# Attention block: the weighted values of every second unit in two halves, and another order of a pair's products

## The chip, the cores and the metric

The kernel runs on one core of one Trainium2 chip. The metric is the device time of one execution in microseconds (us); the time of a kernel is the median of several executions. A second source is one execution under the hardware profiler, which records every instruction with its start, its duration and what it waited for.

## The reference

The input `x` has 2048 rows of 512 values. The reference adds a full softmax attention with 32 heads of 16 channels, and after it a gated mixer:

```python
def _A_ref(x, wqkv, wo):
    H = 32; Dh = D // H
    qkv = (x @ wqkv).reshape(B, S, 3, H, Dh)...
    scores = jnp.einsum("bhqd,bhkd->bhqk", q, k) * Dh ** -0.5
    p = _softmax(scores, axis=-1)
    o = jnp.einsum("bhqk,bhkd->bhqd", p, v)
    return o... @ wo
...
h = x + _A_ref(_layernorm(x, axis=-1), A_wqkv, A_wo)
h2 = h + _B_ref(_layernorm(h, axis=-1), B_w_in, B_w_sp, B_b_sp, B_w_out)
```

Everything is float32. The change touches the attention alone: the scores, the row maxima that the softmax subtracts, and the product of the weights with the values.

## The kernel before

**Stages.** The first stage normalizes `x` and makes queries, keys and values; the second is the attention, which this text is about; then come the product with `wo`, the mixer's first product, its product over the sequence and its last product.

**Units of attention.** Four heads are handled together (a group `hg`, 8 in all), 512 queries at a time (a block `qb`, 4 in all), 128 keys at a time (`kb`, 16 in all). One such piece is a unit; there are 512 units, and the loop at L744 takes two per turn: `kb` even and `kb1`, the odd one behind it. Such a turn is called a pair here, and eight pairs make a block of queries.

**Scores and weights.** `score` (L665) makes the scores of two of the four heads: two TensorE products of 512 columns into one tile `s` of two PSUM banks (L673), and one ScalarE exponential over both banks, into `pt` (L676). The two products stand in different rows of the array: head `t=0` uses rows 0 to 49, `t=1` rows 64 to 113. Products in the upper and in the lower rows can run beside each other. The pool `ps_s` has two tiles, so the third `score` of a pair writes where the first one was, and waits for its exponential.

**Weighted values.** `weigh` (L679) multiplies the weights of the four heads with the values: four products, each with all 128 rows of the array but 32 of its columns, into the four quarters of one PSUM bank `pv`. The operands are plain float32, and the compiler makes two instructions of each, so one `weigh` is eight instructions (L684). The sum over the 16 units of a block stays in `pv`; `gather` (L687) then copies it out, half of it on VectorE (L690) and half on ScalarE (L694), and `weigh` of the next block's first unit has to wait for both copies.

**Maxima.** The softmax needs the maximum of each query's scores ahead of time. `max_pair` (L207) makes them for 128 queries and two heads per pair, eleven pairs (`LEAD`) ahead of their use. It returns eight steps. Each is one product of 512 columns in the upper (`t=0`) or lower (`t=1`) rows into one of three single banks (`ps_m`, numbers 0 to 2), and what reads that bank: six are read by a VectorE maximum (L230), `minus` by a ScalarE absolute value into `ab` (L235), and `plus` by a VectorE custom operation that takes `ab` too (L239). The first four keys' blocks of the upper head are taken through sum and difference, which is why that head has `plus`, `minus` and the blocks 2 and 3 only. Every eighth pair, `last` also reduces the maxima on VectorE (L245), and in the pair behind it `max_rows` (L255) transposes them (L259) and sends them into the query tile by DMA. `invert` (L644, a VectorE reciprocal at L648) runs once in a block.

**Order.** In this part the order of TensorE, ScalarE, VectorE and SyncE is the order of the program (`manual_schedule`, L743). A pair issues, on TensorE (upper, lower: the rows used; the bank of a maximum in brackets):

| place | before |
|---|---|
| 1 | `S0` upper, lower; `Sb` upper, lower (the scores of unit `kb`, both head pairs) |
| 2 | `four0` lower (2), `two` upper (0) |
| 3 | `weigh` of the pair before's second unit |
| 4 | `minus` upper (1), `four1` lower (2) |
| 5 | `Sc` upper, lower; `four2` lower (0); `Sd` upper, lower (the scores of unit `kb1`) |
| 6 | `four3` lower (1), `plus` upper (2) |
| 7 | `weigh` of this pair's first unit |
| 8 | `last` upper (1): block 3 of the upper head |

The names in this table are used from here on; `S0`, `Sb`, `Sc`, `Sd` stand for the four calls of `score`. In the first pair of a block, `gather` is called between 4's two products. From unit 490 on there are no maxima left, and the steps do nothing; products of the next stage (`more_h`) take their place.

Of the kernel before, what the change touches and what calls it, by code (L numbers as in the profile page):

```python
# [8 lines left out]
F32 = mybir.dt.float32  # L9
# [3 lines left out]
AF = mybir.ActivationFunctionType  # L13
# [5 lines left out]
P = 128  # L19
# [3 lines left out]
DH = 16  # L23
# [3 lines left out]
NB = S // P  # L27
HB = NB // 2
NQ = S // 512
DB = D // P  # L30
HG = H // 4
# [17 lines left out]
def block_kernel(ctx: ExitStack, tc: tile.TileContext, x, wqkv, wo, w_in, w_sp4, b_sp, w_out, out):  # L49
# [154 lines left out]
            return more[i]()  # L204
        return ps_m.tile([P, 512], F32, name=f"m{i}")

    def max_pair(m):  # L207

        g, i = divmod(m, 8)
        hg, qb = divmod(g, NQ)
        q, k, w = qst[g], kst[hg % 2], uvs[hg % 2]
        if i == 0:
            mx[g] = sm.tile([P, 16, 4], F32, name="mx")
            nc.gpsimd.memset(mx[g][:, :8, 3:], LOW)
        c, p = slice(i % 4 * P, i % 4 * P + P), i // 4
        at = lambda t, e: mx[g][:, t * 8 + i, e:e + 1]  # L220

        def scores(t, keys, b):
            r = slice(RG * t, RG * t + KS)
            acc = bank(b)
            nc.tensor.matmul(acc, q[r, p, c], keys[r, p], start=True, stop=True)  # L225
            return acc

        def one(t, e, b):
            acc = scores(t, k[:, :, 512 * e:512 * e + 512], b)
            nc.vector.reduce_max(at(t, e if t else e - 1), acc, axis=AX.X)  # L230

        def minus(b):
            acc = scores(0, w[:, :, 512:], b)
            ab[0] = sm.tile([P, 512], F32, name="ab")
            nc.scalar.activation(ab[0], acc, AF.Abs)  # L235

        def plus(b):
            acc = scores(0, w[:, :, :512], b)
            nc.vector.tensor_tensor_reduce(ab[0], acc, ab[0], 0.5, LOW, ALU.add, ALU.max, at(0, 0))  # L239

        def last(b):
            one(0, 3, b)
            if i == 7:
                nm = sm.tile([P, 2, 8], F32, name="nm")
                nc.vector.tensor_reduce(nm.rearrange("p t i -> p (t i)"), mx.pop(g), axis=AX.X,  # L245
                                        op=ALU.max, negate=True)
                parts = sm.tile([P, 2, 2, 8], F32R, name="mparts")
                split(parts[:, :, 0], parts[:, :, 1], nm, "pool", "pool")
                turned[0] = (g, parts)

        ab = {}
        four = [lambda b, e=e: one(1, e, b) for e in range(4)]
        return [four[0], lambda b: one(0, 2, b), minus, four[1], four[2], four[3], plus, last]

    def max_rows():  # L255

# [398 lines left out]
    with ExitStack() as at:  # L655
# [6 lines left out]
        ps_s = at.enter_context(tc.tile_pool(name="ps_s", bufs=2, space=PSUM))  # L662
        pv = {}

        def score(hg, qb, kb, p):  # L665

            q, k = qst[hg * NQ + qb], kst[hg % 2]
            turn[0] += len(later)
            pool = later[0] if later and turn[0] % 3 == 2 else ps_s
            s = pool.tile([P, 2, 512], F32, name="s")  # L670
            for t in range(2):
                r = slice(RG * t, RG * t + KM)
                nc.tensor.matmul(s[:, t, :], k[r, p, kb * P:(kb + 1) * P], q[r, p, :],  # L673
                                 start=True, stop=True)
            t = pp.tile([P, 2, 512], F32, name="pt")
            nc.scalar.activation(t, s, AF.Exp, scale=DH ** -0.5)  # L676
            return t

        def weigh(hg, qb, kb, pts):  # L679
            if kb == 0:  # L680
                pv[0] = ps_v.tile([P, 512], F32, name="pv")
            for j in range(4):
                c = (4 * kb + j) * VW
                nc.tensor.matmul(pv[0][32 * j:32 * j + 32, :], vst[hg % 2][:, c:c + 32],  # L684
                                 pts[j % 2][:, j // 2, :], start=kb == 0, stop=kb == NB - 1)

        def gather(hg, qb, pool=sm):  # L687

            o = pp.tile([P, 512], F32, name="o", bufs=1)
            nc.vector.tensor_copy(o[:, :256], pv[0][:, :256])  # L690
            if pool is sm and later:
                nc.vector.tensor_copy(o[:, 256:], pv[0][:, 256:])
            else:
                nc.scalar.activation(o[:, 256:], pv[0][:, 256:], AF.Copy)  # L694
            cols = slice(qb * 512, (qb + 1) * 512)
            sums = pool.tile([P, 16], F32, name="sums")
            for j in range(4):
                h = head(hg, j % 2, j // 2)
                nc.sync.dma_start(o_scr[h * DH:(h + 1) * DH, cols], o[32 * j:32 * j + DH, :])
                nc.sync.dma_start(sums[32 * j:32 * j + 32, :], o[32 * j + DH:32 * j + VW, :])  # L700
            sums_[0] = (hg, cols, sums, pool)
# [18 lines left out]
        def more_h(k):  # L720

            for _ in range(k):
                if not pieces:
                    sb = h_rows[len(hns)]
                    acc = later[0].tile([P, 512], F32, name="h")
                    pieces.extend([sb, acc, h_products(sb, acc)])
                sb, acc, products = pieces
                next(products)
                made[0] += 1
                if made[0] % (3 * DB):  # L730
                    continue
                pieces.clear()
                add_h(sb, acc)
                split_o(h_rows[len(hns) + 1], *("pool", "pool") if hns else [None])
                mv, rs = scale_h(sb)
                hns[sb] = e2.tile([P, D], F32, name="hn", bufs=3)
                nc.vector.tensor_scalar(hns[sb], xrs.pop(sb), mv[:, 0:1], rs,
                                        op0=ALU.subtract, op1=ALU.mult)
# [4 lines left out]
        with tc.manual_schedule(engines={E.PE, E.Activation, E.DVE, E.SP}):  # L743
            for n in range(0, len(units), 2):  # L744
                (hg, qb, kb), (_, _, kb1) = units[n:n + 2]
                if hg + 1 < HG and n % 64 < 24 and n % 4 == 0:
                    load_k(hg + 1, [n % 64 // 4])
                if hg + 1 < HG and n % 64 < 12 and n % 4 == 2:
                    load_uv(hg + 1, [n % 64 // 4])
                if hg + 1 < HG and n % 64 == 30:  # L750
                    load_v(hg + 1)
                if kb == 2 and n // NB + 3 < HG * NQ:
                    load_q(n // NB + 3)
                steps = max_pair(m) if m < 8 * HG * NQ else []
                m += 1
                if not steps and not later:
                    maxima.close()
                    later.append(attn.enter_context(
                        tc.tile_pool(name="ps_l", bufs=1, space=PSUM, side="right")))
                step = lambda b: steps and steps.pop(0)(b)  # L760
                pts = [score(hg, qb, kb, 0), score(hg, qb, kb, 1)]
                step(2)
                step(0)
                if prev is None:

                    pv[0] = ps_v.tile([P, 512], F32, name="pv")
                    for j in range(4):
                        nc.tensor.matmul(pv[0][32 * j:32 * j + 32, :], vst[0][:, :32],
                                         vst[0][:, :512], start=True, stop=True)
                else:  # L770
                    weigh(*prev)
                step(1)
                if kb == 0 and n:
                    gather(*units[n - 1][:2])
                step(2)
                pts1 = [score(hg, qb, kb1, 0)]
                step(0)
                pts1.append(score(hg, qb, kb1, 1))
                step(1)
                step(2)  # L780
                if n >= 490:
                    more_h(2 + (n < 494))
                weigh(hg, qb, kb, pts)
                if turned:
                    max_rows()
                step(1)
                prev = (hg, qb, kb1, pts1)
                if kb == 6 and n > NB:
                    invert()
                if n % 32 == 16 and n < 6 * 32:  # L790
                    load_weights(n // 32)
                if n in (476, 482, 492, 504):
                    load_o(h_rows[(476, 482, 492, 504).index(n)])
                if n == 482:
                    split_o(h_rows[0], "pool", "pool")
            weigh(*prev)
            gather(*prev[:2], e2)
# [186 lines left out]
    with ExitStack() as fin:  # L984
# [29 lines left out]
        def product(acc, a, b, blocks=range(HB)):  # L1014
            for k in blocks:
                mm3(acc, a[0][:, k, :], a[1][:, k, :], b[0][:, k, :], b[1][:, k, :],
                    k == 0, k == HB - 1)
# [299 lines left out]
```

## Time and profile before

| | us |
|---|---|
| median of 3 runs | 1863.78 (1863.67 to 1863.93) |
| the profiled execution's own time | 1863.55 |
| its span in the profile | 1861.7 |
| first and last absolute value `ab` of the attention loop's 245 pairs with maxima | 170.4 and 1360.2 |
| VectorE busy between 800 and 1000 us | 183.80 of 200 |
| ScalarE busy there | 176.64 of 200 |

The span reaches from the first to the last instruction that the profiler recorded. An engine's busy time counts the time in which at least one of its instructions runs. The TensorE row says little by itself: matmuls overlap, and the ends of those rows are modelled, so the engine seems to be busy all the time. Their starts are recorded, and differences between starts are what the reading goes by. In a timeline, several instructions of a kind that follow one another are one row, with the start of the first and a count; PEld is the loading of a product's weights into the array, ahead of the product.

### The profile page before, as it was taken

The numbers are of one execution on the slowest core, as the hardware profiler recorded it, in microseconds if no ns is written. First come the engines' busy times: TensorE is split into PE (matmuls) and PEld (weight loads), VectorE is DVE, ScalarE is ACT, GpSimd is POOL, SyncE is SP. The second block draws the span as 40 slices with busy tenths as digits, with TensorE's granted clock in tenths as the row PEclk, the third lists the DMA queues.
The fourth block names the chain that finished last, engine by engine and source line by source line (L and its number), as shares of the span: only waits on it lengthen the run. The fifth ranks groups of instructions, "written<-read, shape, count | busy, mean of one in ns | idle before, by whom it ended". The sixth has DMA issues, their size and how long they took to land.

```text
span 1861.7 us, 31964 instructions
## 1 busy us (share of the span) xinstructions
PE 1852.8 (100%) x11410; PEld 1047.3 (56%) x11410; DVE 1530.4 (82%) x3060; ACT 1317.8 (71%) x1696; POOL 225.7 (12%) x305
## 2 busy tenths in 40 slices
PE   9999999999999999999999999999999999999999
PEld 6775444444444444444444444444437889999998
DVE  6487999999999999999999999999935766877664
ACT  3224888888888888888888888888895444434221
POOL 2241000011010100000000000000001756001111
PEclk9999999999999999999999999999999999999999
DMA  6688111221120121022011112100123555768662
GB/s 192 193 191 197 41 24 30 48 53 28 39 57 15 49 44 25 13 51 40 13 39 32 23 29 50 25 14 13 30 56 108 175 160 166 226 186 264 212 191 94
DMA packets 148743, 159.90 MB, mean 86 GB/s; under 512 B 63096, under 2 KB 93320, under 8 KB 147240
## 3 DMA queue, kind: packets, MB, share of 16 engines
q1 hardware_dynamic: 143800, 146.44, 29.7%
q10 hardware_dynamic: 4752, 11.41, 1.6%
q8 instruction: 90, 1.47, 0.3%
q14 instruction: 69, 0.57, 0.1%
q0 software_dynamic: 32, 0.01, 0.0%
HBM read 101.26 MB, written 55.61 MB: 84 GB/s over the span
## 4 chain that ended last, share of the span: by engine, by line
PE 98%; DVE 1%; issue 0%; ACT 0%; DMA 0%; SPq 0%; POOL 0%; POOLq 0%; DVEq 0%; ACTq 0%
PE pv L684 27%; PE m L225 26%; PE s L673 13%; PE acc L96 5%; PE acc L98 5%; PE acc L97 5%; PE g L98 4%; PE g L97 4%; PE g L96 4%; PE acc L617 2%; PE tp L1189 1%; PE h L617 0%; PE tp L885 0%; PE acc L1210 0%; PE tp L369 0%
## 5 line engine op out<-in xcount | busy, mean ns | idle before, releaser
L676 ACT ACTIVATE pt<-s 128x1024 f32<-128x1024 f32 x1024 | 994.1, 1030 | 141.6 <-PE s L673 139.2
L230 DVE TENSOR_REDUCE mx<-m 128x1 f32<-128x512 f32 x1508 | 956.6, 684 | 99.7 <-PE m L225 56.6
L225 PE MATMUL m<-kst,qst 48*128 48x512 f32 x1508 | 605.1, 447 | 0.0
L684 PE MATMUL pv<-pt,vst 128*32 128x512 f32 x4096 | 545.8, 605 | 0.0
L673 PE MATMUL s<-qst,kst 50*128 50x512 f32 x2048 | 465.1, 428 | 0.0
L225 PEld LDWEIGHTS m<-kst,qst 48*128 48x128 f32 x1508 | 262.7, 184 | 316.2 <-DVE mx L230 221.4
L673 PEld LDWEIGHTS s<-qst,kst 50*128 50x128 f32 x2048 | 222.6, 185 | 53.9 <-ACT pt L676 29.8
L225 PE MATMUL m<-uvs,qst 48*128 48x512 f32 x497 | 246.5, 496 | 0.0
L225 PEld LDWEIGHTS m<-uvs,qst 48*128 48x128 f32 x497 | 90.8, 183 | 205.4 <-DVE mx L230 204.6
L684 PEld LDWEIGHTS pv<-pt,vst 128*32 128x32 f32 x4096 | 80.8, 108 | 158.2 <-issue 155.5
L239 DVE CUSTOM_DVE_ANT_0 ab<-m,ab 128x512 f32<-128x512 f32 x249 | 169.6, 681 | 0.0
L235 ACT ACTIVATE ab<-m 128x512 f32<-128x512 f32 x248 | 149.3, 602 | 4.1 <-PE m L225 4.0
L90 POOL CAST mparts<-nm 128x16 fp32r<-128x16 f32 x32 | 6.3, 197 | 880.2 <-DVE nm L245 880.2
L825 ACT ACTIVATE ws<-a 128x512 fp32r<-128x512 f32 x80 | 45.8, 621 | 50.0 <-PE g L98 23.6
L904 ACT ACTIVATE z<-acc 128x464 f32<-128x464 f32 (+2 forms) x64 | 27.6, 456 | 65.3 <-PE acc L98 63.3
L96 PE MATMUL acc<-wi,hT 128*128 128x464 f32 (+2 forms) x196 | 72.8, 371 | 0.0
L98 PE MATMUL acc<-wi,hT 128*128 128x464 f32 (+2 forms) x196 | 71.8, 366 | 0.0
L97 PE MATMUL acc<-wi,hT 128*128 128x464 f32 (+2 forms) x196 | 71.6, 365 | 0.0
L826 DVE TENSOR_TENSOR ws<-a,ws 128x512 fp32r<-128x512 f32 x80 | 56.1, 745 | 13.1 <-ACT ws L825 13.0
L96 PE MATMUL g<-b,ws 128*128 128x344 f32 x192 | 62.6, 326 | 0.0
L88 ACT ACTIVATE part<-acc 128x512 fp32r<-128x512 f32 x32 | 19.1, 598 | 60.8 <-PE acc L98 56.0
L98 PE MATMUL g<-t,ws 128*128 128x344 f32 x192 | 61.3, 319 | 0.0
(200 smaller groups left out, 2121.2 us busy)
## 6 DMA issues: line engine op xcount, KB each, us to landing
a<-in_w_sp SPq DMA_DIRECT2D x80, 256.0 KB
qst<-q_scr SPq DMA_DIRECT2D x192, 64.0 KB
z_scr<-z ACTq DMA_DIRECT2D x32, 344.0 KB
kst<-k_scr SPq DMA_DIRECT2D x42, 256.0 KB
k_scr<-part SPq DMA_DIRECT2D x16, 512.0 KB
q_scr<-part SPq DMA_DIRECT2D x16, 512.0 KB
z<-z_scr SPq DMA_DIRECT2D x14, 344.0 KB
b<-z_scr SPq DMA_DIRECT2D x24, 172.0 KB
```

The lines of the kernel that those rows point to most:

```text
L96: nc.tensor.matmul(ps, lh, rh, start=first, stop=False)
L97: nc.tensor.matmul(ps, lh, rl, start=False, stop=False)
L98: nc.tensor.matmul(ps, ll, rh, start=False, stop=last)
L225: nc.tensor.matmul(acc, q[r, p, c], keys[r, p], start=True, stop=True)
L230: nc.vector.reduce_max(at(t, e if t else e - 1), acc, axis=AX.X)
L235: nc.scalar.activation(ab[0], acc, AF.Abs)
L239: nc.vector.tensor_tensor_reduce(ab[0], acc, ab[0], 0.5, LOW, ALU.add, ALU.max, at(0, 0))
L673: nc.tensor.matmul(s[:, t, :], k[r, p, kb * P:(kb + 1) * P], q[r, p, :], start=True, stop=True)
L676: nc.scalar.activation(t, s, AF.Exp, scale=DH ** -0.5)
L684: nc.tensor.matmul(pv[0][32 * j:32 * j + 32, :], vst[hg % 2][:, c:c + 32], pts[j % 2][:, j // 2, :], start=kb == 0, stop=kb == NB - 1)
L825: nc.scalar.activation(hi, src, AF.Copy)
L826: (nc.gpsimd if el == "pool" else nc.vector).tensor_sub(lo, src, hi.bitcast(F32))
```

## The change

`max_pair` gets an argument `late`, with which it returns the same eight products in another order, with `four3` as the last one in place of the upper head's block 3 (here `last`). `score` is taken apart into `scores_of`, which returns two functions: the first makes the upper product, the second the lower product and the exponential. `weigh` takes a range of columns. The loop's body, for pairs that have maxima, is written anew; for the others it is as before, without the empty steps. What a pair issues on TensorE becomes:

| place | after |
|---|---|
| 1 | `minus` upper (2); `S0` upper, lower; `four0` lower (1); `Sb` upper |
| 2 | `weigh` of the pair before's second unit, columns 0 to 255 (all columns in the first pair of a block) |
| 3 | `two` upper (0); `Sb` lower; `last` upper (1); `four1` lower (2); `Sc` upper, lower |
| 4 | `weigh` of the same unit, columns 256 to 511 (nothing in the first pair of a block) |
| 5 | `Sd` upper; `four2` lower (0); `plus` upper (1); `Sd` lower |
| 6 | `weigh` of this pair's first unit, whole |
| 7 | `four3` lower (0) |

`gather` now stands between `last` and `four1`. VectorE's order in a pair becomes `four0`, `two`, `last`, `four1`, `four2`, `plus`, `four3` (before: `four0`, `two`, `four1`, `four2`, `four3`, `plus`, `last`), and ScalarE's becomes `minus`, `S0`, `Sb`, `Sc`, `Sd` (before: `S0`, `Sb`, `minus`, `Sc`, `Sd`).

```diff
-    def max_pair(m):
+    def max_pair(m, late=False):
...
-        return [four[0], lambda b: one(0, 2, b), minus, four[1], four[2], four[3], plus, last]
+        two = lambda b: one(0, 2, b)
+        if late:
+            return [minus, four[0], two, lambda b: one(0, 3, b), four[1], four[2], plus,
+                    lambda b: last(b, 1, 3)]
+        return [four[0], two, minus, four[1], four[2], four[3], plus, lambda b: last(b, 0, 3)]
...
-        def weigh(hg, qb, kb, pts):
+        def weigh(hg, qb, kb, pts, cols=slice(0, 512)):
...
-                nc.tensor.matmul(pv[0][32 * j:32 * j + 32, :], vst[hg % 2][:, c:c + 32],
-                                 pts[j % 2][:, j // 2, :], start=kb == 0, stop=kb == NB - 1)
+                nc.tensor.matmul(pv[0][32 * j:32 * j + 32, cols], vst[hg % 2][:, c:c + 32],
+                                 pts[j % 2][:, j // 2, cols], start=kb == 0,
+                                 stop=kb == NB - 1 and cols.stop == 512)
...
-                pts = [score(hg, qb, kb, 0), score(hg, qb, kb, 1)]
-                step(2)
-                step(0)
...
-                    weigh(*prev)
-                step(1)
-                if kb == 0 and n:
-                    gather(*units[n - 1][:2])
-                step(2)
-                pts1 = [score(hg, qb, kb1, 0)]
-                step(0)
-                pts1.append(score(hg, qb, kb1, 1))
-                step(1)
-                step(2)
...
-                weigh(hg, qb, kb, pts)
-                if turned:
-                    max_rows()
-                step(1)
+                if steps:
+                    step = lambda b: steps.pop(0)(b)
+                    step(2)
+                    pts = [score(hg, qb, kb, 0)]
+                    step(1)
+                    first, second = scores_of(hg, qb, kb, 1)
+                    first()
...
+                        weigh(*prev, *[slice(0, 256)] * (kb > 0))
+                    step(0)
+                    pts.append(second())
+                    step(1)
+                    if kb == 0 and n:
+                        gather(*units[n - 1][:2])
+                    step(2)
+                    pts1 = [score(hg, qb, kb1, 0)]
+                    if kb:
+                        weigh(*prev, slice(256, 512))
+                    first, second = scores_of(hg, qb, kb1, 1)
+                    first()
+                    step(0)
+                    step(1)
+                    pts1.append(second())
+                    weigh(hg, qb, kb, pts)
+                    if turned:
+                        max_rows()
+                    step(0)
```

More of the change, by code (lines that the diff above doesn't have):

```diff
@@ L239, in plus, with last @@
             nc.vector.tensor_tensor_reduce(ab[0], acc, ab[0], 0.5, LOW, ALU.add, ALU.max, at(0, 0))
-        def last(b):
-            one(0, 3, b)
+        def last(b, *which):
+            one(*which, b)
             if i == 7:
@@ L663, in block_kernel, with score, scores_of @@
         pv = {}
-        def score(hg, qb, kb, p):
+        def score(*unit):
+            first, second = scores_of(*unit)
+            first()
+            return second()
+        def scores_of(hg, qb, kb, p):
             q, k = qst[hg * NQ + qb], kst[hg % 2]
@@ L670, in score, with product @@
             s = pool.tile([P, 2, 512], F32, name="s")
-            for t in range(2):
+            def product(t):
                 r = slice(RG * t, RG * t + KM)
@@ L674, in score, with second @@
                                  start=True, stop=True)
-            t = pp.tile([P, 2, 512], F32, name="pt")
-            nc.scalar.activation(t, s, AF.Exp, scale=DH ** -0.5)
-            return t
-        def weigh(hg, qb, kb, pts):
+            def second():
+                product(1)
+                t = pp.tile([P, 2, 512], F32, name="pt")
+                nc.scalar.activation(t, s, AF.Exp, scale=DH ** -0.5)
+                return t
+            return lambda: product(0), second
+        def weigh(hg, qb, kb, pts, cols=slice(0, 512)):
             if kb == 0:
@@ L753, in block_kernel @@
                     load_q(n // NB + 3)
-                steps = max_pair(m) if m < 8 * HG * NQ else []
+                steps = max_pair(m, True) if m < 8 * HG * NQ else []
                 m += 1
@@ L759, in block_kernel @@
                         tc.tile_pool(name="ps_l", bufs=1, space=PSUM, side="right")))
-                step = lambda b: steps and steps.pop(0)(b)
-                pts = [score(hg, qb, kb, 0), score(hg, qb, kb, 1)]
-                step(2)
-                step(0)
[L764 to L769, printed above, removed]
+                if steps:
[5 more added lines that the diff above has]
+                    first()
+                    if prev is None:
+                        pv[0] = ps_v.tile([P, 512], F32, name="pv")
+                        for j in range(4):
+                            nc.tensor.matmul(pv[0][32 * j:32 * j + 32, :], vst[0][:, :32],
+                                             vst[0][:, :512], start=True, stop=True)
+                    else:
+                        weigh(*prev, *[slice(0, 256)] * (kb > 0))
[9 more added lines that the diff above has]
+                    first, second = scores_of(hg, qb, kb1, 1)
+                    first()
+                    step(0)
[5 more added lines that the diff above has]
+                    step(0)
@@ L770, in block_kernel @@
                 else:
+                    pts = [score(hg, qb, kb, 0), score(hg, qb, kb, 1)]
                     weigh(*prev)
-                step(1)
-                if kb == 0 and n:
-                    gather(*units[n - 1][:2])
-                step(2)
-                pts1 = [score(hg, qb, kb1, 0)]
-                step(0)
-                pts1.append(score(hg, qb, kb1, 1))
-                step(1)
-                step(2)
-                if n >= 490:
-                    more_h(2 + (n < 494))
@@ L783, in block_kernel @@
-                weigh(hg, qb, kb, pts)
-                if turned:
-                    max_rows()
-                step(1)
+                    if kb == 0:
+                        gather(*units[n - 1][:2])
+                    pts1 = [score(hg, qb, kb1, 0), score(hg, qb, kb1, 1)]
+                    if n >= 490:
+                        more_h(2 + (n < 494))
+                    weigh(hg, qb, kb, pts)
+                    if turned:
+                        max_rows()
                 prev = (hg, qb, kb1, pts1)
```

## The prediction

> **What bounds the kernel now.** I read the page first.
>
> ```profile
> PE 1852.8 (100%) x11410; PEld 1047.3 (56%) x11410; DVE 1530.4 (82%) x3060; ACT 1317.8 (71%) x1696; POOL 225.7 (12%) x305
> PE 98%; DVE 1%; issue 0%; ACT 0%; DMA 0%; SPq 0%; POOL 0%; POOLq 0%; DVEq 0%; ACTq 0%
> L676 ACT ACTIVATE pt<-s 128x1024 f32<-128x1024 f32 x1024 | 994.1, 1030 | 141.6 <-PE s L673 139.2
> L230 DVE TENSOR_REDUCE mx<-m 128x1 f32<-128x512 f32 x1508 | 956.6, 684 | 99.7 <-PE m L225 56.6
> L684 PE MATMUL pv<-pt,vst 128*32 128x512 f32 x4096 | 545.8, 605 | 0.0
> ```
>
> The chain of waits says 98% TensorE, which is no finding: the matmul rows overlap. So I took the stage between 800 and 1000 us, by stretches and then by the timeline of each engine. All three engines are nearly full, and none quite:
>
> ```profile
> 800.00:1000.00 200.00, 200.00 (x1314) 82.60 (x1312) 183.80 (x349) 176.64 (x211) 3.37 (x16) 1.00 0.17 36
> ```
>
> The columns are the stretch, its length, then busy us and instructions of PE, PEld, DVE, ACT, POOL, then the granted clock (full), the DMA share and GB/s. TensorE, in order of time:
>
> ```profile
> 800.72 1.06 PE L684 MATMUL pv<-pt,vst 128*32 128x512 f32 x8
> 801.72 0.50 PE L225 MATMUL m<-kst,qst 48*128 48x512 f32 x1
> 801.72 0.96 PE L673 MATMUL s<-qst,kst 50*128 50x512 f32 x4
> 802.34 0.58 PE L225 MATMUL m<-kst,qst 48*128 48x512 f32 x2
> 802.85 1.07 PE L684 MATMUL pv<-pt,vst 128*32 128x512 f32 x8
> 803.85 0.50 PE L225 MATMUL m<-uvs,qst 48*128 48x512 f32 x1
> 803.85 0.49 PE L225 MATMUL m<-kst,qst 48*128 48x512 f32 x1
> 804.19 0.40 PE L673 MATMUL s<-qst,kst 50*128 50x512 f32 x2
> 804.42 0.40 PE L225 MATMUL m<-kst,qst 48*128 48x512 f32 x1
> 804.55 0.51 PE L673 MATMUL s<-qst,kst 50*128 50x512 f32 x2
> 805.04 0.50 PE L225 MATMUL m<-kst,qst 48*128 48x512 f32 x1
> 805.17 0.49 PE L225 MATMUL m<-uvs,qst 48*128 48x512 f32 x1
> 805.59 1.06 PE L684 MATMUL pv<-pt,vst 128*32 128x512 f32 x8
> ```
>
> A pair takes 805.59 - 800.72 = 4.87 us: `weigh` 1.00, the row-half products `last` to `two` 1.13, `weigh` 1.00, the products `minus` to `plus` 1.74. Upper and lower products start side by side (803.85 twice). Behind a first product the next in the same rows comes after 0.34 us (803.85 to 804.19), each further one after 0.24 (804.19 to 804.42); `weigh` starts 0.42 behind a lone first product (805.17 to 805.59). A stage of k products in the busier rows so takes 0.10 + 0.24k + 0.08: 1.14 for the four upper ones of the first stage (measured 1.13), 1.38 for the five lower ones of the second, where 1.74 are seen. The 0.36 us between are waits, and the other engines' rows name them:
>
> ```profile
> 804.55 0.19 PEld L673 LDWEIGHTS s<-qst,kst 50*128 50x128 f32 x2 [0.17 <-ACT pt L676]
> 805.04 0.18 PEld L225 LDWEIGHTS m<-kst,qst 48*128 48x128 f32 x1 [0.30 <-ACT ab L235]
> 805.16 0.18 PEld L225 LDWEIGHTS m<-uvs,qst 48*128 48x128 f32 x1
> 802.56 1.94 ACT L676 ACTIVATE pt<-s 128x1024 f32<-128x1024 f32 x2 [0.61 <-PE s L673]
> 803.48 1.02 ACT L676 ACTIVATE pt<-s 128x1024 f32<-128x1024 f32 x1
> 804.38 0.60 ACT L235 ACTIVATE ab<-m 128x512 f32<-128x512 f32 x1
> 804.88 1.94 ACT L676 ACTIVATE pt<-s 128x1024 f32<-128x1024 f32 x2
> 802.25 1.89 DVE L230 TENSOR_REDUCE mx<-m 128x1 f32<-128x512 f32 x3 [0.20 <-PE s L673]
> 804.42 1.89 DVE L230 TENSOR_REDUCE mx<-m 128x1 f32<-128x512 f32 x3 [0.28 <-PE m L225]
> 806.22 0.68 DVE L239 CUSTOM_DVE_ANT_0 ab<-m,ab 128x512 f32<-128x512 f32 x1
> ```
>
> `four1` starts at 803.85, its maximum at 804.42 (0.57 later), which ends near 805.11, and `plus`, which wants the bank, loads at 805.16. So today's loop is: `weigh`, `four1`, its maximum, `plus`, `weigh`, the first stage; 1.00 + 0.57 + 0.69 + 0.05 + 0.42 + 1.00 + 1.13 = 4.86, against 4.87 seen. The same steps also give what I need below: a first product's reader starts 0.53 behind it (`minus` 803.85, `ab` 804.38), a maximum follows another after 0.60 (three in 1.89), an exponential starts 0.50 behind a score product that had its rows warm (`S0` upper at 801.72 + 0.34 = 802.06, exponential 802.56), so 0.60 behind a first one; it ends after 1.02 (803.48 to 804.50), and the waiting product loads 0.05 later (804.55).
>
> **The change part by part.** *The new order of the products* removes one upper or lower product's time: stages of three, three and two products in the busier rows (`four3` beside `minus`, `S0` upper beside lower, `four0` beside `Sb` upper; and so on) instead of four and five. That is 8 x 0.24 in place of 9 x 0.24. *The split* adds eight instructions in each of 214 pairs (245 less the 31 first ones of a block) and one more change between full-row and half-row products, 0.10 + 0.08. *Both* also move who waits for whom, which decides.
>
> A half `weigh` has no row in this trace. The nearest are products by columns and, for the kinds of the extra VectorE work, these (line, shape, count, busy us and mean ns):
>
> ```profile
> L98 PE MATMUL acc<-xT,wqk 128*128 128x512 f32 x128 | 49.9, 390 | 0.0
> L98 PE MATMUL g<-t,ws 128*128 128x344 f32 x192 | 61.3, 319 | 0.0
> L690 DVE COPY o<-pv 128x256 f32<-128x256 f32 x15 | 6.2, 415 | 0.0
> L648 DVE RECIPROCAL rcp<-sums 128x16 f32<-128x16 f32 x15 | 3.6, 243 | 0.0
> L245 DVE TENSOR_REDUCE nm<-mx 128x16 f32<-128x64 f32 x16 | 3.5, 220 | 0.5
> ```
>
> 168 columns less are 71 ns less, 0.42 ns per column and pass. An instruction of `weigh` is 605 - 390 = 215 ns longer than a one-pass product of 512 columns, which is one more pass (512 x 0.42 = 216). Two instructions behind one another make four passes, 0.87 of `weigh`'s 1.00 us, and 256 columns less save 4 x 256 x 0.42 = 0.43. I take **0.57** for a half. Its bounds: 0.45 if a half is worth its streaming only, without the drain and fill around it; 1.00 if columns save nothing.
>
> The drain is where the Trainium skill speaks against the change. The row: `weigh` starts 0.42 behind `plus`, though 0.34 is all that a next product in those rows would have waited. The page "TensorEngine Tiling (Array Packing)", section "Key Properties", says that changing the tiling mode, and not merely the tile, drains the engine. By that rule the third change per pair costs its 0.18 in each of 214 pairs, 39 us of TensorE's time; without it the rival with 0.45 below would hold. The trace agrees with the rule so far as it goes.
>
> Now the loop after, from the start of `four3` and `minus` (0.00), in an ordinary pair. `S0` 0.34, `four0` and `Sb` upper 0.58, half `weigh` from 0.90 (three products: 0.10 + 0.72 + 0.08) to 1.47. `two` and `Sb` lower at 1.47. From here two ways lead on. (a) The exponential of `Sb` can't start before its lower product, which now stands behind the half: 1.47 + 0.60 = 2.07, ends 3.09; `Sd` wants that tile and loads at 3.14. (b) `four3`'s maximum starts at 0.53, `four0`'s at 1.13, ends 1.82; `last` wants its bank and comes at 1.87, `four1` queued behind it too; a stage of two, 0.66, leads to the second half at 2.53, which ends at 3.10. So `Sd`, `four2`, `plus` start at 3.14; a stage of two to 3.80; `weigh` to **4.80**. The same walk gave 0.01 too little for before, so 4.81: **0.06 us saved** in an ordinary pair. TensorE's own work would be 0.90 + 0.57 + 0.90 + 0.57 + 0.66 + 1.00 = 4.60; waits eat 0.20 of it.
>
> What is late next: *the first pair of a block* keeps `weigh` whole, and way (a) runs through all of it: 1.00 - 0.57 = **+0.43**. *The extra VectorE work* meets a chain that it didn't meet before: today `four0` and `two` have some 0.3 us to spare ahead of `four1`; now `four3`, `four0` and `last` follow each other on way (b), 0.04 shorter than (a). The reciprocal (0.243, queued between `four3` and the next `four0`) costs 0.20, the reduction at L245 in the same place 0.18, and `gather`'s copy, ahead of `four1`, makes `four2`, `plus` and the next `four3` late. There `two` comes at 1.90, its maximum at 2.43, `last`'s at 3.03, the copy at 3.63, `four1`'s at 4.0, `four2`'s at 4.6, ending at 5.29; so `four3` comes at 5.34 instead of 5.23, and its own maximum behind `plus` (5.2 + 0.76) at 5.96 instead of 5.76: 0.20 less the 0.04 to spare, about 0.17. The transpose stands behind `plus`, which ends at about 5.16, with 0.17 us free ahead of `four3`'s maximum at 5.33: hidden; its cost without that would be 0.2. Together **+0.55** a block.
>
> The DMAs are the same and keep their places but for `gather`'s eight, which SyncE issues a little later in the pair; `weigh` doesn't wait for them, and the queues move 36 GB/s here, so nothing. From unit 490 on the order is unchanged: nothing.
>
> Sum: the attention's pairs now take, extra work included, (1360.2 - 170.4)/244 = 4.876, so 39.01 for eight; after, 8 x 4.81 + 0.43 + 0.55 = 39.46. The 245 pairs are 30.6 blocks: 30.6 x 0.45 = **+13.8 us**. On the profiled 1863.55 that is 1877.4; the median is 0.23 above it, so **1878 us**.
>
> ```profile
> L235 ACT ACTIVATE ab<-m x248: 597/602/605, 104.2 to 1360.2; 128x512 f32<-128x512 f32 x124
> 170.38 0.60 ACT L235 ACTIVATE ab<-m 128x512 f32<-128x512 f32 x1 [0.48 <-PE m L225]
> ```
>
> **The rivals.** *The half is cheap (0.45).* If the drain is not paid around a half, (a) gives `Sb` lower at 1.35, its exponential held by ScalarE's own queue till about 1.96, `Sd` at 3.03, and the pair 4.70; the first pair of a block is then 0.54 dearer than that, the extra work about 0.5: 8 x 4.70 + 1.04 = 38.64, -0.37 a block, -11 us: **1852**, the other side. The point from which it decides is a half of 0.50. For it: streaming alone is halved surely. Against: each of the changes in the timeline shows the 0.18.
>
> *The half is dear.* Loading weights for eight more instructions might not hide behind passes half as long. At 0.75, (a) has `Sd` at 3.32 and (b) at 3.28, so the pair takes 0.18 more, 39 us in 214 pairs: near **1916**. At the bound of 1.00, (b) has three products between the halves, 1.90 + 0.90 + 1.00 = 3.80, which is 0.66 a pair, 141 us: near 2020. Against: the loads of `weigh` overlap each other and the products (eight of both within its 1.06 us).
>
> *The extra work is hidden.* If VectorE's additions find slack after all, 245 x 0.065 are saved and 31 x 0.43 paid: -3 us, **1861**, which a measurement here can hardly tell from no change (0.2%, 3.7 us, is about what it can). For it: today they are nearly hidden.
>
> *TensorE's own 4.60 is reached,* because the exponential of `Sb` is not on the path: 214 x 0.27 less, some 1820. Against: two tiles for four scores; `Sd` has nowhere else to go.
>
> **How the numbers follow.** The forecast, slower by the first pair of a block and the late VectorE work, 0.68 (0.55 to 0.60 for a half moves a block by -0.14 to +0.21, 0.3 to 0.7 for the extras by -0.25 to +0.15: 1866 to 1889); dear half 0.08; hidden extras 0.08, within 0.2%; cheap half 0.13 and TensorE's own time 0.03, both faster. So faster 0.16, same 0.08, slower 0.76. The range 1857 to 1894 holds the forecast, the hidden extras and a little of the dear and cheap sides, 0.8 in all.
>
> **What would show it.** In the profile after: `weigh`'s rows of 256 columns, with 0.57 from their first start to the next product's; ordinary pairs 4.81 apart by the rows of `ab`, the first of a block about 5.2, and two or three others near 5.0; waits of `Sd` for ScalarE's `pt` and of `last` for VectorE's maximum, in place of those of `four3` for `ab`. The prediction is wrong if a half takes 0.50 or less, if the exponential of `Sb` starts earlier than 0.6 behind the half's end, or if the first pair of a block is no longer than the others.

## The result and the profile after

| | us |
|---|---|
| before, median of 6 runs beside it | 1863.81 |
| after, median of 6 runs | 1893.11 (1892.97 to 1893.35) |
| ratio after/before | 1.0157, interval 1.0144 to 1.0170 |
| span of the profiled execution, after | 1891.5 (before 1861.7) |

The changed kernel is 29.3 us slower; 14 were forecast. The page after:

```profile
PE 1843.6 (97%) x13122; PEld 1005.5 (53%) x13122; DVE 1529.9 (81%) x3060; ACT 1362.0 (72%) x1696; POOL 225.3 (12%) x305
PE 89%; DVE 5%; ACT 3%; issue 1%; SPq 0%; DMA 0%; DVEq 0%; POOL 0%; POOLq 0%; ACTq 0%
PE pv L703 27%; PE m L225 19%; PE s L686 13%; PE acc L96 5%; PE acc L98 5%; PE acc L97 5%; DVE mx L230 4%; PE g L98 4%; PE g L97 3%; PE g L96 3%; PE acc L621 2%; ACT pt L692 2%; ACT o L714 1%; DVE o L710 1%; PE tp L1227 0%
```

TensorE has 1712 instructions more (13122 - 11410), eight in each of 214 pairs, and VectorE does what it did. The chain of waits is worth reading now: it runs through VectorE and ScalarE for 8% of the span, and two lines stand in it that run once in a block, `gather`'s copies at L710 and L714. So work that is done once in eight pairs has come onto the path.

The starts of `ab`, one per pair, show which pairs are long. This is ScalarE's timeline of the changed kernel, its L235 alone, over one block:

```profile
567.74 0.60 ACT L235 ACTIVATE ab<-m 128x512 f32<-128x512 f32 x1 [0.34 <-PE m L225]
573.34 0.62 ACT L235 ACTIVATE ab<-m 128x512 f32<-128x512 f32 x1
578.45 0.60 ACT L235 ACTIVATE ab<-m 128x512 f32<-128x512 f32 x1 [0.34 <-PE m L225]
583.29 0.60 ACT L235 ACTIVATE ab<-m 128x512 f32<-128x512 f32 x1 [0.34 <-PE m L225]
588.14 0.60 ACT L235 ACTIVATE ab<-m 128x512 f32<-128x512 f32 x1 [0.35 <-PE m L225]
593.02 0.60 ACT L235 ACTIVATE ab<-m 128x512 f32<-128x512 f32 x1 [0.34 <-PE m L225]
598.05 0.60 ACT L235 ACTIVATE ab<-m 128x512 f32<-128x512 f32 x1 [0.34 <-PE m L225]
602.89 0.60 ACT L235 ACTIVATE ab<-m 128x512 f32<-128x512 f32 x1 [0.35 <-PE m L225]
```

From row to row: 5.60, 5.11, 4.84, 4.85, 4.88, 5.03, 4.84. Means of such distances over 29 blocks of each trace, by the place of the pair in its block:

| pair | 1 | 2 | 3 | 4 | 5 | 6 | 7 | 8 | block |
|---|---|---|---|---|---|---|---|---|---|
| before | 4.96 | 4.87 | 4.86 | 4.86 | 4.86 | 4.86 | 4.86 | 4.88 | 39.01 |
| after | 5.61 | 5.11 | 4.84 | 4.84 | 4.88 | 5.03 | 4.83 | 4.84 | 39.98 |

A block is 0.97 us longer, and 30.6 blocks are the whole 29.6: nothing went anywhere else. Ordinary pairs are 0.02 shorter, the first pair and three others longer.

An ordinary pair, TensorE's timeline of the changed kernel (rows between left out), and then two weight loads (PEld) of the same stretch with their waits:

```profile
802.22 0.50 PE L225 MATMUL m<-kst,qst 48*128 48x512 f32 x1
802.23 0.50 PE L225 MATMUL m<-uvs,qst 48*128 48x512 f32 x1
803.12 0.64 PE L703 MATMUL pv<-pt,vst 128*32 128x256 f32 x8
803.69 0.50 PE L225 MATMUL m<-kst,qst 48*128 48x512 f32 x1
803.69 0.50 PE L686 MATMUL s<-qst,kst 50*128 50x512 f32 x1
804.78 0.64 PE L703 MATMUL pv<-pt,vst 128*32 128x256 f32 x8
806.07 1.07 PE L703 MATMUL pv<-pt,vst 128*32 128x512 f32 x8
```

```profile
804.10 0.19 PEld L225 LDWEIGHTS m<-kst,qst 48*128 48x128 f32 x2 [0.23 <-DVE mx L230]
805.39 0.18 PEld L686 LDWEIGHTS s<-qst,kst 50*128 50x128 f32 x1 [0.45 <-ACT pt L692]
```

From `four3` and `minus` at 802.22: the first half of `weigh` at 0.90 (forecast 0.90), the products behind it at 1.47 (1.47, so a half takes 0.57), `last` at 1.88 behind VectorE's maximum (1.87), the second half at 2.56 (2.53), `Sd` at 3.17 behind ScalarE's exponential (3.14), the whole `weigh` at 3.85 (3.80). Three products and a half, three and a half, two and a whole: the order, the price of a half and both waits are as the walk had them.

The first pair of a block and the start of the second, changed kernel, all engines (rows between left out):

```profile
807.06 0.50 PE L225 MATMUL m<-kst,qst 48*128 48x512 f32 x1
807.96 1.06 PE L703 MATMUL pv<-pt,vst 128*32 128x512 f32 x8
808.96 0.50 PE L686 MATMUL s<-qst,kst 50*128 50x512 f32 x1
809.59 1.02 ACT L692 ACTIVATE pt<-s 128x1024 f32<-128x1024 f32 x1 [0.44 <-PE s L686]
810.66 0.49 PE L686 MATMUL s<-qst,kst 50*128 50x512 f32 x1 [0.74 <-ACT pt L692]
810.70 0.41 DVE L710 COPY o<-pv 128x256 f32<-128x256 f32 x1
811.14 0.38 ACT L714 ACTIVATE o<-pv 128x256 f32<-128x256 f32 x1 [0.54 <-DVE o L710]
811.50 1.94 ACT L692 ACTIVATE pt<-s 128x1024 f32<-128x1024 f32 x2
811.67 1.06 PE L703 MATMUL pv<-pt,vst 128*32 128x512 f32 x8 [0.27 <-ACT o L714]
812.67 0.49 PE L225 MATMUL m<-kst,qst 48*128 48x512 f32 x1
813.20 1.29 DVE L230 TENSOR_REDUCE mx<-m 128x1 f32<-128x512 f32 x2 [0.29 <-PE m L225]
813.50 0.18 PEld L686 LDWEIGHTS s<-qst,kst 50*128 50x128 f32 x1 [0.30 <-ACT pt L692]
```

`Sb` lower at 1.90 and `Sd` at 3.60 from the start (forecast 1.90 and 3.57). VectorE's copy starts at 3.64 (forecast 3.63). Then comes what the forecast left out: ScalarE's copy of the other columns of `pv` is released by VectorE's copy and runs from 4.08 to 4.46, and `weigh` waits for it until 4.61 (4.54 in the mean of 29 blocks); by the forecast it would have started at 4.23. Before, the same two copies had their places too, but the second was hidden, because ScalarE was busy with `ab` until long after VectorE had copied, and `weigh` came later than both:

```profile
833.34 0.41 DVE L690 COPY o<-pv 128x256 f32<-128x256 f32 x1
833.64 0.60 ACT L235 ACTIVATE ab<-m 128x512 f32<-128x512 f32 x1
834.12 0.40 ACT L694 ACTIVATE o<-pv 128x256 f32<-128x256 f32 x1
834.83 1.06 PE L684 MATMUL pv<-pt,vst 128*32 128x512 f32 x8
```

The second pair, which starts at 812.67, is long for the same copy, one step further on. The exponentials of `Sc` and `Sd` stand behind ScalarE's copy and run from 811.50 to 813.44; the next `Sb` wants `Sd`'s tile, and its upper product loads at 813.50, 0.83 behind the start of the pair. In an ordinary pair it comes at 0.57. VectorE isn't late here: it sits idle for 0.29 ahead of `four3`'s maximum, which starts 0.53 behind its product, as in every pair. In the mean of 29 blocks `Sb`'s upper product comes 0.24 late and the half `weigh` 0.34, as it starts 0.43 behind a product that has waited and 0.33 behind one that hasn't. By the starts of the products the first pair takes 5.54 and the second 5.18, which is these 0.34 more than an ordinary one; the table has 5.61 and 5.11 because the second pair's `ab` is itself 0.07 late.

### The profile page after: what moved, and what is told of

Its sections match the earlier page's. It is cut to its first block, busy times and chain, and to the rows that moved or that the text cites. A ratio compares the mean times of both kernels' runs of the same rounds, so it can differ in the third digit from the quotient of the medians.

```text
span 1891.5 us, 35579 instructions
## 1 busy us (share of the span) xinstructions
PE 1843.6 (97%) x13122; PEld 1005.5 (53%) x13122; DVE 1529.9 (81%) x3060; ACT 1362.0 (72%) x1696; POOL 225.3 (12%) x305
## 4 chain that ended last, share of the span: by engine, by line
PE 89%; DVE 5%; ACT 3%; issue 1%; SPq 0%; DMA 0%; DVEq 0%; POOL 0%; POOLq 0%; ACTq 0%
PE pv L703 27%; PE m L225 19%; PE s L686 13%; PE acc L96 5%; PE acc L98 5%; PE acc L97 5%; DVE mx L230 4%; PE g L98 4%; PE g L97 3%; PE g L96 3%; PE acc L621 2%; ACT pt L692 2%; ACT o L714 1%; DVE o L710 1%; PE tp L1227 0%
## 5 line engine op out<-in xcount | busy, mean ns | idle before, releaser
L692 ACT ACTIVATE pt<-s 128x1024 f32<-128x1024 f32 x1024 | 1017.5, 1023 | 36.0 <-PE s L686 22.8
L686 PE MATMUL s<-qst,kst 50*128 50x512 f32 x2048 | 580.5, 424 | 27.5 <-ACT pt L692 27.5
L703 PE MATMUL pv<-pt,vst 128*32 128x256 f32 (+1 forms) x5808 | 591.3, 479 | 6.1 <-ACT o L714 5.9
L225 PE MATMUL m<-kst,qst 48*128 48x512 f32 x1508 | 568.1, 470 | 5.4 <-DVE mx L230 4.8
L225 PEld LDWEIGHTS m<-kst,qst 48*128 48x128 f32 x1508 | 225.9, 184 | 387.0 <-DVE mx L230 352.7
L686 PEld LDWEIGHTS s<-qst,kst 50*128 50x128 f32 x2048 | 275.1, 185 | 176.1 <-ACT pt L692 144.2
L703 PEld LDWEIGHTS pv<-pt,vst 128*32 128x32 f32 x5808 | 114.6, 108 | 241.5 <-issue 227.8
L225 PE MATMUL m<-uvs,qst 48*128 48x512 f32 x497 | 221.3, 445 | 0.0
L235 ACT ACTIVATE ab<-m 128x512 f32<-128x512 f32 x248 | 148.7, 600 | 77.5 <-PE m L225 77.5
```

Source lines behind the costliest of these rows:

```text
L703: nc.tensor.matmul(pv[0][32 * j:32 * j + 32, cols], vst[hg % 2][:, c:c + 32], pts[j % 2][:, j // 2, cols], start=kb == 0, stop=kb == NB - ...
```

## The experiments

Two theories of what the forecast lacked. The copies: the first pair's `weigh` waits for ScalarE's copy, which waits for VectorE's, which stands behind two maxima. The whole product: the first pair is long because `weigh` is whole there, and the copies run beside that.

**e1, one copy, on ScalarE.**

```diff
-            nc.vector.tensor_copy(o[:, :256], pv[0][:, :256])
...
+            if pool is sm and not later:
+                nc.scalar.activation(o, pv[0], AF.Copy)
```

> The changed kernel, with gather's copy of pv made by ScalarE alone (one copy of 512 columns in place of 256 on VectorE and 256 on ScalarE) while maxima are being made. Theory of the copies: in the first pair of a block the whole weigh of the pair waits for ScalarE's copy, and that waits for VectorE's copy, which stands behind two maxima; with one copy on ScalarE the first pair falls from 5.61 to about 5.25 us, a block from 39.98 to about 39.5, the kernel by some 15 us to 1878. Theory of the whole product: the first pair is long because weigh stands whole ahead of Sb's exponential, and the copies are beside that; then the first pair keeps its 5.6 us and the kernel its 1893.

Measured: 1881.1 us, ratio to before 1.0091 (1.0076 to 1.0107). First pair 5.27, second 5.02, block 39.56. ScalarE's and TensorE's timeline of e1 in a first pair:

```profile
841.41 1.06 PE L703 MATMUL pv<-pt,vst 128*32 128x512 f32 x8
843.04 1.02 ACT L692 ACTIVATE pt<-s 128x1024 f32<-128x1024 f32 x1 [0.44 <-PE m L225]
843.96 0.59 ACT L711 ACTIVATE o<-pv 128x512 f32<-128x512 f32 x1
844.11 0.49 PE L686 MATMUL s<-qst,kst 50*128 50x512 f32 x1 [0.73 <-ACT pt L692]
844.78 1.07 PE L703 MATMUL pv<-pt,vst 128*32 128x512 f32 x8
```

From the first `weigh` to the second 3.37 instead of 3.71 (807.96 to 811.67): the copy ends at 844.55 and nothing waits for it: `weigh` comes 0.67 behind `Sd` (844.11), as far as in an ordinary pair. What is left of the first pair, 5.27 against 4.84, is the 0.43 that the forecast had for the whole product. The theory of the copies holds, and the other does for its own part. The second pair stays long: ScalarE's longer copy still stands ahead of the exponentials of `Sc` and `Sd`, and `Sb`'s upper product comes 0.66 behind that pair's start (845.78 to 846.44). In e2 and e6 below, whose second pair is not long, it comes at 0.57.

**e2, the copies first.** `gather` is called behind the whole `weigh`, ahead of `two`:

```diff
                         weigh(*prev, *[slice(0, 256)] * (kb > 0))
+                    if kb == 0 and n:
+                        gather(*units[n - 1][:2])
                     step(0)
                     pts.append(second())
                     step(1)
-                    if kb == 0 and n:
-                        gather(*units[n - 1][:2])
```

> The changed kernel, with gather called right behind the whole weigh of a block's first pair, ahead of two, Sb's lower product and last, so that VectorE copies before it takes those two maxima. Theory of the copies: nothing waits for the copies any longer, but both maxima are 0.33 us later; the first pair about 5.52 us, and the second, 5.11 in the changed kernel, about 4.84; a block 39.56, the kernel some 13 us faster, 1880. Theory of the whole product: first and second pair as they are, 1893, or worse by the later maxima (two, last and all behind them), about 1898.

Measured: 1881.83 us, ratio 1.0095 (1.0079 to 1.0112); first pair 5.50, second 4.83. VectorE's timeline of e2, then ScalarE's:

```profile
565.62 0.42 DVE L710 COPY o<-pv 128x256 f32<-128x256 f32 x1 [0.22 <-PE pv L703]
```

```profile
566.08 0.38 ACT L714 ACTIVATE o<-pv 128x256 f32<-128x256 f32 x1 [0.42 <-DVE o L710]
566.36 2.96 ACT L692 ACTIVATE pt<-s 128x1024 f32<-128x1024 f32 x3
```

VectorE copies at once, ScalarE's copy is out of the way of the exponentials of `Sc` and `Sd`, and the second pair's delay is gone. But ScalarE's copy still waits for VectorE's, and now the exponential of `Sb` waits behind it, until 566.36. This is the same wait with another victim: the first pair gains 0.10 where e1's gains 0.34.

**e3, the order without the halves.**

```diff
-                        weigh(*prev, *[slice(0, 256)] * (kb > 0))
+                        weigh(*prev)
...
-                    if kb:
-                        weigh(*prev, slice(256, 512))
```

> The new order of the products alone: every weigh whole, at the place of the first half. Theory that the pair is set by the exponential of Sb behind the half product (Sb's lower product, exponential, Sd, weigh): every pair gets what the first pair of a block has from it, 0.43 us more, about 5.25 to 5.3, and the kernel 80 us slower than the changed one, 1975. Rival, that the third change between row-half and full-row products is what costs: taking it away saves 0.18 to 0.19 us a pair less the waits that it uncovers, and the kernel is at 1855 to 1870.

Measured: 1977.5 us, ratio 1.0609 (1.0593 to 1.0624), ordinary pairs 5.26. TensorE and ScalarE of e3 in such a pair:

```profile
804.24 1.06 PE L703 MATMUL pv<-pt,vst 128*32 128x512 f32 x8
805.24 0.50 PE L686 MATMUL s<-qst,kst 50*128 50x512 f32 x1
805.86 2.96 ACT L692 ACTIVATE pt<-s 128x1024 f32<-128x1024 f32 x3 [0.44 <-PE s L686]
806.94 0.50 PE L686 MATMUL s<-qst,kst 50*128 50x512 f32 x1 [0.72 <-ACT pt L692]
807.60 1.07 PE L703 MATMUL pv<-pt,vst 128*32 128x512 f32 x8
```

`Sb` lower behind the whole `weigh`, exponential 0.62 later, `Sd` 1.08 behind that, `weigh` 0.66 on. There is one change less between full-row and half-row products, and the pair is 0.42 longer: what sets the pair is the way through that exponential, and the halves are what makes the new order bearable at all.

**e4, the halves without the order.** The kernel before, with

```diff
-                    weigh(*prev)
+                    halves = kb > 0 and len(steps) > 0
+                    weigh(*prev, *[slice(0, 256)] * halves)
...
                 pts1 = [score(hg, qb, kb1, 0)]
+                if prev is not None and halves:
+                    weigh(*prev, slice(256, 512))
                 step(0)
```

> The kernel before, with weigh of the pair before's second unit in two halves (not in the first pair of a block): the first half where weigh stood, the second behind the two products of Sc; all else in the order of before. If a half costs 0.57 us and the third change is paid, and the stage behind it still waits for ab and the maxima of four1, the pair goes from 4.87 to about 5.1 and the kernel to about 1930. If the halves hide in the 0.36 us that the second stage of before waits anyway, the kernel stays within 10 us of before, 1855 to 1875.

Measured: 1911.83 us, ratio 1.0256 (1.0241 to 1.0271), ordinary pairs 5.00: between the two numbers, nearer the first. TensorE's timeline of e4, then a weight load in it:

```profile
802.71 0.64 PE L684 MATMUL pv<-pt,vst 128*32 128x256 f32 x8
803.28 0.50 PE L225 MATMUL m<-uvs,qst 48*128 48x512 f32 x1
803.71 0.49 PE L225 MATMUL m<-kst,qst 48*128 48x512 f32 x1
804.37 0.64 PE L684 MATMUL pv<-pt,vst 128*32 128x256 f32 x8
```

```profile
803.71 0.18 PEld L225 LDWEIGHTS m<-kst,qst 48*128 48x128 f32 x1 [0.25 <-DVE mx L230]
```

A half again takes 0.57 (802.71 to 803.28). Coming 0.43 earlier than a whole one ends, it lets `minus` start, but `four1` waits for VectorE's maximum of `four0` all the same; the half's gain is waited away, and the second half and its change between full-row and half-row products remain to be paid. Each part alone is slower than before, the order by 113 us and the halves by 48; together 29.

**e5, the reciprocal behind `plus`.** `invert()` is called before the second product of `Sd` instead of at the end of the pair.

> The changed kernel, with the reciprocal of invert queued on VectorE behind plus instead of behind four3. Theory that VectorE work between four3 and four0 delays last, and that work behind plus finds it free: of the two pairs near 5.0 us in a block one (5.03, if the reciprocal makes it) falls to 4.84 or so, 4 us less in all, 1889. Rival, that VectorE's extra work costs the same wherever it stands: 1893.

Measured: 1892.0 us, ratio 1.0152 (1.0138 to 1.0165). It is the pair of 4.88 that falls, to 4.835; that of 5.03 stays. I had the two the wrong way round. VectorE's timeline of the changed kernel says which is which:

```profile
588.11 0.69 DVE L230 TENSOR_REDUCE mx<-m 128x1 f32<-128x512 f32 x1 [0.29 <-PE m L225]
588.72 0.24 DVE L652 RECIPROCAL rcp<-sums 128x16 f32<-128x16 f32 x1
588.88 3.19 DVE L230 TENSOR_REDUCE mx<-m 128x1 f32<-128x512 f32 x5
...
592.99 0.69 DVE L230 TENSOR_REDUCE mx<-m 128x1 f32<-128x512 f32 x1 [0.32 <-PE m L225]
593.71 0.22 DVE L245 TENSOR_REDUCE nm<-mx 128x16 f32<-128x64 f32 x1
593.85 3.24 DVE L230 TENSOR_REDUCE mx<-m 128x1 f32<-128x512 f32 x5
```

From `four3`'s maximum to `four0`'s it is 0.77 with the reciprocal between, 0.86 with the reduction, against 0.60 without either. The reduction, 0.22 long, costs 0.26, because it starts only when the maximum ahead of it is over (592.99 + 0.69 is 593.68); the reciprocal follows before that (588.72) and costs 0.17. The forecast for the kernel, 4 us less, was too much: it is 1.1. No run moved the reduction.

**e6, `Sb` lower and the copies ahead of `two`.**

```diff
-                    step(0)
                     pts.append(second())
+                    if kb == 0 and n:
+                        gather(*units[n - 1][:2])
+                    step(0)
                     step(1)
-                    if kb == 0 and n:
-                        gather(*units[n - 1][:2])
```

> The changed kernel, with Sb's lower product and its exponential, and gather behind them, issued ahead of two. By the walk of the copies (VectorE copies before two, as in e2, and ScalarE's exponential of Sb isn't held up by its copy) and of the exponential (it no longer waits for two's record): the first pair near 5.2, the second 4.84, the ordinary ones 4.79 to 4.84; the kernel 1868 to 1876. If the order of those two products, which start side by side in different rows, is of no account, it does what e2 does: 1882.

Measured: 1868.91 us, ratio 1.0029 (1.0019 to 1.0040). First pair 5.23, second 4.81, ordinary ones 4.80. This is 24 us of the 29. The first two pairs are 0.68 a block, 21 us; the ordinary ones, 0.03 each, the rest. Both copies are still made: ScalarE's starts 0.95 behind the end of VectorE's, behind the exponential of `Sb`, and ends 0.45 ahead of `weigh`, so nobody waits for either.

**e7, before with two maxima earlier.** In the kernel before, `four0` and `two` are issued between the scores `S0` and `Sb`:

```diff
-                pts = [score(hg, qb, kb, 0), score(hg, qb, kb, 1)]
+                pts = [score(hg, qb, kb, 0)]
                 step(2)
                 step(0)
+                pts.append(score(hg, qb, kb, 1))
```

> The kernel before, with four0 and two issued between S0 and Sb instead of behind both; nothing else. VectorE then has their maxima 0.24 us earlier, so that gather's copy and the reduction fall into time that it has free: the first pair of a block falls from 4.96 towards 4.87, the others stay, 4 to 6 us less in all, 1858 to 1860. If what the first pair of before costs is not VectorE's lateness, or if Sb's later exponential is felt, nothing is gained: 1864 or more.

Measured: 1860.14 us against 1863.65, ratio 0.9981 (0.9973 to 0.9990). First pair 4.84 instead of 4.96, the others as they were, as forecast. This version is faster than both kernels; by which wait, no run took apart.

**e8, e5 and e6 together.**

> e5 and e6 together: the changed kernel with the copies, the product and the reciprocal moved. If the parts are what the walk makes of them, they add up: a block near 39.05 to 39.3, the kernel 1865 to 1873, about before's time, with the whole product in the first pair (0.4 us in each of 31) as what is left to pay against the 0.03 to 0.07 saved in the ordinary pairs. Rival: the parts overlap, and it is no faster than e6.

Measured: 1866.73 us, ratio 1.0017 (1.0009 to 1.0026), block 39.09. The parts add up (e5's 1.1 and e6's 24.2 give 25.3 of 29.3; 26.4 measured: the pair with the reciprocal falls by 0.07 here and by 0.045 in e5, which is most of the difference), and the changed order is back within 0.2% of before. Of what is left, the first pair is 5.23 and the one with the reduction 5.03, while ordinary pairs are 4.805 against 4.86.

## Why the prediction had the ordinary pairs and only half of the cost

- **What bounds the kernel now, and the walk along the order:** right. The same walk gave 4.80 for the ordinary pair after (4.84 measured) and, ahead of e3, 5.25 to 5.3 for the pair there (5.26).
- **A half at 0.57:** right, in the changed kernel and in e4. So both rivals of a cheap and a dear half fall: of 1.00 us, 0.43 were saved, as the columns alone would have it, and the rest, 0.13 of a whole one, is in the half too (0.14). The Trainium skill says that a change of the tiling mode drains the engine ("TensorEngine Tiling (Array Packing)", "Key Properties"). That this rest is such a drain agrees with these numbers, but no run here shows it apart from another fixed cost.
- **The ordinary pair at 4.81:** 4.84. The exponential of `Sb` starts a little later than 0.60 behind its product (0.62 in the mean of the ordinary pairs, 0.63 in the first pair above, 808.96 to 809.59); e6, where that product stands ahead of `two` in the queue, has 4.80. Over a block this term is 0.22 short.
- **The first pair, +0.43 for the whole `weigh`:** right by itself; e1 leaves exactly that (5.27 against 4.84).
- **`gather`'s copy, "about 0.17": this is the step that failed.** It was costed as VectorE's copy alone, by its delay of later maxima, and ScalarE's copy was put at nothing without a reason. That the second copy waits for the first, and the whole `weigh` for both, wasn't followed to its end, though the walk had the first copy's start right to 0.01. Measured: the first pair 5.61, 0.34 above e1's, and the second 0.27 above an ordinary one, 0.61 in place of 0.17. None of it comes by way of the maxima that stand behind VectorE's copy. In the first pair `weigh` waits for ScalarE's copy, and in the second `Sb` waits for an exponential that was queued behind that copy. e6, with both copies but without these waits, leaves 5.23 for the first pair, which is its ordinary 4.80 and the 0.43, and 4.81 for the second.
- **The reciprocal 0.20 and the reduction 0.18:** 0.04 and 0.19. The spare time between the ways (a) and (b) was right: in the mean ordinary pair the second half ends at 2.56 + 0.57 = 3.13, and `Sd` comes at 3.17. The reduction makes `four0`'s maximum 0.25 late and the second half 0.23, of which 0.19 are felt. The reciprocal was taken nearly at its length; it makes the maximum 0.16 late, but the second half only 0.09, of which 0.05 are felt (e5 gains 0.045). The transpose is hidden, as said.
- **The sum:** a block +0.45 forecast, +0.97 measured: +0.22 from the ordinary pairs, +0.44 from the copies, -0.15 from the reciprocal and the reduction. The extra work of a block came to 0.84, outside its bounds of 0.3 to 0.7; that 1893 lies just inside the range of 1857 to 1894 is owed to the range's width and not to the walk.
- **The rival of hidden extra work:** false; that of TensorE's own 4.60 too: `Sd` waits for ScalarE in every ordinary pair.

What stays open: why ScalarE's copy waits for VectorE's. Both read the same bank and write different columns of one tile. The trace shows the release, in each of 30 blocks 0.03 behind the end of VectorE's copy, and not the reason; no run makes the two copies read different banks or write different tiles.

## What to carry to other kernels

Where an order is packed tighter, list everything that happens once per several turns, and follow each such piece to whoever waits for it last: here three short operations and one wait between two copies, once in eight turns, cost more than the packing saved in all eight. A wait that was hidden before has to be looked for in the program, as it can be missing among the waits of the trace: in the kernel before, the row of ScalarE's copy (834.12) names no wait for VectorE's. And before work is moved behind a long product, ask which engine's next step begins with it: the halves had to be there because an exponential had been put behind them.

## What the runs showed of the hardware

Two products in different rows that start at the same time don't release their readers at the same time: with `two` ahead of `Sb` in the queue the exponential starts 0.62 behind the common start and `two`'s maximum 0.53; with `Sb` issued first (e6) it is 0.59 and 0.56, and the pair is 0.03 us shorter, with nothing else changed in ordinary pairs (4.84 to 4.80). Small operations on VectorE don't cost their length: 0.22 us of reduction took 0.26, as it waits for the operation before it, and 0.24 us of reciprocal took 0.17, and 0.04 of the pair.
